# Where the block sums and the high and low parts of w1 and w2 are made: at the conversion, in the second and third pair, instead of in the first group of the last stage

## The chip, the cores and the metric

The kernel runs on one core of a Trainium2 chip. The metric is the device time of one execution in microseconds (us). PE is TensorE, DVE is VectorE, ACT is ScalarE, POOL is GpSimd, and SP is SyncE, which here issues nearly all DMAs. A piece is called 128x512 when it has 128 partitions with 512 numbers in each.

## The reference, cut to what matters

Three blocks follow one another. The weights arrive as 64 bit floats and are converted in the kernel.

```python
attn = sm_attn(q, sm_attn(p, k, v), same)     # 8 batches, 8 heads, 576 rows, 64 wide; 32 packed rows
x = attn.transpose(0, 2, 1, 3).reshape(4608, 512)
x = (silu(x @ w_gate) * (x @ w_val)) @ w_out  # d_ff = 1536
h = (x @ w1) * (x @ w2) @ w3                  # w1, w2: 512 x 1024; w3: 1024 x 1024
out = h @ w_out2                              # 4608 x 512
```

## The kernel before, in words

Every matmul operand is held as a high part (rounded by a cast on ACT) and a low part (value minus high part, a subtraction on DVE or POOL), and three products are added. `split` (L89 and L93) does this.

**Pairs.** After the packed attention, the eight batches go in four pairs P = 0 to 3. A pair runs over 12 feature blocks f of 128. In a step (P, f), `c_mm` multiplies the next step's weights with the packed values into a PSUM tile pc (L409); ACT copies it rounded to ch (L420), and DVE subtracts ch from pc to get cl (L89). `stage1` then makes, for each of the two batches, pg (L441; silu on ACT, L446) and pv (L441; u = u times pv on DVE, L450). Each u is cast to uh on ACT, and POOL subtracts to get ul. After each third f, `stage3` multiplies three f with w_out into px (L672), in two halves that lie inside the next step; without them a step is short. So a short step on PE is pc, pg, pv, pg', pv' (the prime is for the second batch). The PSUM tiles of this part come from one pool of four, in turn: pv' of a step takes the place that pc of the same step had, and so it can start only when the DVE subtraction cl has read pc.

DVE and ACT also work out the softmax of the next pair's queries in these steps (`q_tasks`: sT, qmx, qsm, aT, aTl, transposes qT), and the conversions of weights to 32 bits (`conv`: ACT L346, DVE L347 and L350).

**w1 and w2.** Sixteen conversions i = 0 to 15 stand at the end of the steps from P = 1, f = 3 to P = 2, f = 6. Before, each takes a 128x512 piece of w1 or w2 (`w12_conv`) and stores it to `w12d`.

**The last stage.** Six groups g of tokens are done; each has eight `stage5(g, f)` and a `stage7(g)`. A `stage5` forms x2 @ w1 and x2 @ w2 of one f by seven products of blocks instead of eight (`PROD`): the weight blocks A11, A12, A22 and four sums S1 to S4 of them, against blocks and sums of x2. A step of seven products uses seven tiles `ws`. Before, group 0 makes them: it loads the converted weights (`load_w12`), forms the sums on DVE (`ws_sums`), splits them on ACT and on DVE or POOL (`ws_block`), and stores the tiles to `wsd`, from where groups 1 to 5 load them (`ws_load`). The results of the products go from PSUM to s by ACT (L996).

**Order.** Each engine runs its own fixed list, written when the program is built; an engine waits at the first instruction that isn't ready. Some instructions are pinned behind others (`pin`). SP's list holds the DMA issues, also in one order. Every tile pool has a fixed number of places, and a write waits for the last reader of the place. Raw weights come through a ring of five tiles (tag `raw`), filled by `raw_load`.

Of the kernel before, what the change touches and what calls it, by code (L numbers as in the profile page):

```python
# [8 lines left out]
F32 = mybir.dt.float32  # L9
F32R = mybir.dt.float32r  # L10
I32 = mybir.dt.int32
I64 = mybir.dt.int64
AF = mybir.ActivationFunctionType
ALU = mybir.AluOpType
# [12 lines left out]
S1 = (14.75, 17.75)  # L27
# [11 lines left out]
def packed_attention_moe_kernel(  # L39
# [24 lines left out]
    nc = tc.nc  # L64
# [26 lines left out]
    def split(hi, lo, src, on="act", sub_on="dve"):  # L91
        if on == "act":
            nc.scalar.copy(hi, src)  # L93
        else:
            nc.vector.tensor_copy(hi, src)
        sub(lo, src, hi, sub_on)
# [1 line left out]
    X2d = tc.dram_tile([ND, 128, NT], F32, name="X2d")  # L98
    Wd = tc.dram_tile([NF, 128, 4, 2, 128], F32, name="Wd")
    wod = tc.dram_tile([NF, 128, DM], F32, name="wod")  # L100
    w12d = tc.dram_tile([NF2, 128, 2, ND, 128], F32, name="w12d")
    wsd = tc.dram_tile([NF2, 7, 128, 2, 2, 128], F32, name="wsd")
    wo3d = tc.dram_tile([2, NF2, 128, DM], F32, name="wo3d")

# [174 lines left out]
        }.get(n - at, lambda: None)()  # L279


    w12_list = [(x, c, h) for h in range(2) for x in range(2) for c in range(ND)]
    NH = NF2 // 2
    raw_q = [f"w_{f}_{gv}" for f in range(4) for gv in range(2)]
    for f in range(NF):
# [9 lines left out]
    def raw_src(key):  # L295
        what, *at = key.split("_")
        at = [int(x) for x in at]
        if what == "wo2":
            c, kk = divmod(at[0], NH)
            return w_out2[512 * c:512 * c + 512, :].rearrange("(i k a) n -> k i a n", k=NH, a=32)[kk]  # L300
        if what == "w3":
            c, r = at
            return w3[128 * r:128 * r + 128, 512 * c:512 * c + 512].rearrange(
                "(b rr) (i n) -> i b rr n", rr=4, i=4)
        if what == "w":
            return (w_gate, w_val)[at[1]][:, 128 * at[0]:128 * at[0] + 128].rearrange(
                "(k p) n -> p k n", p=128)
        if what == "wo":
            return w_out[128 * at[0]:128 * at[0] + 128, :]
        x, c, h = w12_list[at[0]]  # L310
        return (w1, w2)[x][128 * c:128 * c + 128, 512 * h:512 * h + 512]

    raw_at = [0]
    load_after = {}
# [2 lines left out]
    def raw_load():  # L317
        if raw_at[0] < len(raw_q):
            key = raw_q[raw_at[0]]
            src = raw_src(key)  # L320
            raw_at[0] += 1
            blocks = src.shape[0] == 4
            t = vc.tile([128, 512] if blocks else [128] + list(src.shape[1:]), I64, tag="raw",
                        name=f"raw_{key}", bufs=5)
            if blocks:
                for i in range(4):
                    to = t[32 * i:32 * i + 32]
                    nc.sync.dma_start(to if len(src.shape) == 3 else to.rearrange("p (r n) -> p r n", r=4), src[i])
            else:
                nc.sync.dma_start(t, src)  # L330
            raw_t.append((key, t))

    def conv(key, t):


        name, raw = raw_t.pop(0)
        assert name == key, (name, key)
        x = vc.tile(list(t.shape), I32, tag="vx", name=f"vx_{key}")
        w = raw.bitcast(I32)
        if len(t.shape) == 3:  # L340
            w = w.rearrange("p a (n e) -> p a n e", e=2)
            low, high = w[:, :, :, 0], w[:, :, :, 1]
        else:
            w = w.rearrange("p (n e) -> p n e", e=2)
            low, high = w[:, :, 0], w[:, :, 1]
        behind(nc.scalar.activation(t, high.bitcast(F32), AF.Prelu, scale=2.0 ** -112, alpha=-2.0 ** 32), "act")  # L346
        behind(nc.vector.tensor_scalar(x, low, 29, None, op0=ALU.logical_shift_right), "dve")  # L347

        def rest():
            nc.vector.scalar_tensor_tensor(  # L350
                t.bitcast(I32), t.bitcast(I32), 3, x, op0=ALU.logical_shift_left, op1=ALU.bitwise_or)

        if in_front[0]:
            conv_rest.append(rest)
        else:
            rest()
        if not in_front[0]:
            raw_load()


    wf_t, wst_t = {}, {}
# [329 lines left out]


    def w12_conv(i):
        x, c, h = w12_list[i]
        t = vl.tile([128, 512], F32, tag="vu", name=f"w12t{i}")
        conv(f"w12_{i}", t)
        nc.sync.dma_start(
            w12d[4 * h:4 * h + 4, :, x, c, :].rearrange("f p n -> p f n"),
            t.rearrange("p (f n) -> p f n", n=128))


    wo2_t, w3T = {}, {}
# [42 lines left out]
    def w3_step(new, old):  # L745
        if old is not None:
            w3_mm(old)
        if new is not None:
# [5 lines left out]

    PROD = (("A", "A11", "B11"), ("B", "S1", "T1"), ("A", "S2", "T2"), ("B", "S4", "B22"),
            ("A", "S3", "T3"), ("C", "A12", "B21"), ("A", "A22", "T4"))
    x2_t, x2r_t, w12r_t, wsrc, ws_t, wg_at = {}, {}, {}, {}, {}, []

    def load_w12(f):
        t = xp.tile([128, 2, 2, 256], F32, tag="wf", name=f"w12r{f}")  # L760
        nc.sync.dma_start(t.rearrange("p x k n -> p x (k n)"), w12d[f].rearrange("p x c n -> p x (c n)"))
        w12r_t[f] = t

    def ws_sums(f):
        t = w12r_t.pop(f)
        a11, a12, a21, a22 = (t[:, x, kh] for x in range(2) for kh in range(2))
        sa = vl.tile([128, 2, 256], F32, tag="vu", name=f"wsa{f}")
        sb = vl.tile([128, 2, 256], F32, tag="vu", name=f"wsb{f}")
        tt = nc.vector.tensor_tensor
        tt(out=sa[:, 0], in0=a21, in1=a22, op=ALU.add)  # L770
        tt(out=sa[:, 1], in0=sa[:, 0], in1=a11, op=ALU.subtract)
        tt(out=sb[:, 0], in0=a11, in1=a21, op=ALU.subtract)
        tt(out=sb[:, 1], in0=a12, in1=sa[:, 1], op=ALU.subtract)
        wsrc[f] = {"A11": a11, "A12": a12, "A22": a22, "S1": sa[:, 0], "S2": sa[:, 1],
                   "S3": sb[:, 0], "S4": sb[:, 1]}

    def ws_tile(g, f, k):
        if f == 0:
            if k % 2 == 0:
                wg_at.append(wgv.tile([128, 2, 2, 256], F32R, tag=("wh", "wl")[k // 2 % 2], name=f"ws0_{k}"))  # L780
            t = wg_at[-1][:, k % 2]
        else:
            t = wst.tile([128, 2, 256], F32R, tag="wst", name=f"ws{g}_{f}_{k}", bufs=14)
        ws_t[f, k] = t
        return t

    def ws_block(f, k):

        t = ws_tile(0, f, k)
        split(t[:, 0], t[:, 1], wsrc[f][PROD[k][1]], sub_on="pool" if k % 2 else "dve")  # L790
        if f:
            nc.sync.dma_start(wsd[f, k], t.bitcast(F32).rearrange("p h (d n) -> p h d n", d=2))

    def ws_load(g, f, k):
        t = ws_tile(g, f, k)
        nc.sync.dma_start(t.bitcast(F32).rearrange("p h (d n) -> p h d n", d=2), wsd[f, k])

    def x2_load(g, i, j):
        t = xp.tile([128, 2, TH], F32, tag="x2r", name=f"x2r{g}_{i}{j}", bufs=3)
# [57 lines left out]
    for n, (P, f) in enumerate(steps):  # L857
# [46 lines left out]
        if 0 <= i < len(w12_list):  # L904
            pin.update(pin_at)
            w12_conv(i)
            pin.clear()
        if P + 1 < NPR:
            q_tasks(2 * P + 2, 0, f)
            q_tasks(2 * P + 3, 5, f)  # L910
# [6 lines left out]
        if P == NPR - 1:  # L917
            if f == 0:
                aA.release()
                qp.release()  # L920
                wp = pool("wp", "left", bufs=2)
            w3_task(P, f, 3)
            if f == 9:
                assert w3_at[0] > len(w3_list)
                wp.release()
                vc.release()
                xp = pool("xp", "left", bufs=2)
                x2_prep(0, 0)
            if f == 10:
                x2_prep(0, 1)  # L930
                x2_prep(0, 2)
            if f == 11:
                x2_prep(0, 3)
                load_w12(0)
                ws_sums(0)
                for k in range(7):
                    ws_block(0, k)
    for e in range(2):
        stage3(*pend, e)
        if e == 0:  # L940
            load_w12(1)
            ws_sums(1)
            load_w12(2)
    up.release()
    aB.release()
    wop.release()
# [24 lines left out]
    def stage5(g, f):  # L971
# [12 lines left out]

        def ahead(k):

            if g == 0 and f + 1 < NF2:
                ws_block(f + 1, k)
            n = (NF2 - 1) * g + f + 1
            ng, nf = divmod(n, NF2 - 1)  # L990
            if f and 0 < ng < NG2:
                ws_load(ng, nf + 1, k)

        def keep(name, t):
# [54 lines left out]
            nc.sync.dma_start(out[r0:r0 + 128, :], o)  # L1049

    load_wo3(0)
    with tc.manual_schedule(engines=M0):
        for g in range(NG2):
            for f in range(NF2):
                stage5(g, f)
                if g == 0:
                    if f + 2 < NF2:
                        ws_sums(f + 2)
                    if f + 3 < NF2:
                        load_w12(f + 3)  # L1060
                    split_wo3(f)
                    if f + 1 < NF2:
                        load_wo3(f + 1)
            ab_split.pop()()
            if g + 1 < NG2:
                for part in range(4):
                    x2_prep(g + 1, part)
            stage7(g)
# [39 lines left out]
```

## Time and profile before

| | |
|---|---|
| median of 3 runs | 1379.38 us (1378.85 to 1380.13) |
| the profiled execution's own time | 1378.52 us |
| its span in the trace | 1376.7 us |
| mean granted TensorE clock | 0.995 of full |
| busy share of PE, DVE, ACT, POOL | 98%, 48%, 42%, 28% |

By the trace the pairs run from about 120 to 825 us (P = 1 begins near 265, P = 3 near 570), and the last stage from 825 us to the end. The time of the profiled execution has 1.8 us outside the span. A busy share is an average: an engine that is busy for 48% of the span can be without a gap for 20 us, and the others may wait for it there.

### The profile page before, as it was taken

The numbers are of one execution on the slowest core, as the hardware profiler recorded it, in microseconds if no ns is written. First come the engines' busy times: TensorE is split into PE (matmuls) and PEld (weight loads), VectorE is DVE, ScalarE is ACT, GpSimd is POOL, SyncE is SP. The second block draws the span as 40 slices with busy tenths as digits, with TensorE's granted clock in tenths as the row PEclk, the third lists the DMA queues.
The fourth block names the chain that finished last, engine by engine and source line by source line (L and its number), as shares of the span: only waits on it lengthen the run. The fifth ranks groups of instructions, "written<-read, shape, count | busy, mean of one in ns | idle before, by whom it ended". The sixth has DMA issues, their size and how long they took to land.

```text
span 1376.7 us, 25585 instructions
## 1 busy us (share of the span) xinstructions
PE 1344.1 (98%) x10196; PEld 1235.3 (90%) x10196; DVE 658.7 (48%) x962; ACT 572.3 (42%) x956; POOL 386.0 (28%) x309
## 2 busy tenths in 40 slices
PE   6889999999999999999999999999999999999998
PEld 4669899999999999999898989989899899898997
DVE  2875867346563466462354378733413333234230
ACT  4784644235432444344544136433323233233231
POOL 0323322323322233253443226502112022021120
PEclk9999999999999999999999999999999999999999
DMA  9997766534455444145343238928548367285441
GB/s 281 314 268 212 228 188 200 153 97 133 125 127 181 124 135 123 55 144 148 120 130 104 82 121 308 347 70 254 173 131 254 105 198 231 74 253 170 132 152 46
DMA packets 195335, 230.28 MB, mean 167 GB/s; under 512 B 71056, under 2 KB 128400, under 8 KB 195216
## 3 DMA queue, kind: packets, MB, share of 16 engines
q1 hardware_dynamic: 195216, 228.64, 53.8%
q8 instruction: 81, 1.33, 0.4%
q14 instruction: 38, 0.31, 0.1%
HBM read 179.04 MB, written 49.55 MB: 166 GB/s over the span
## 4 chain that ended last, share of the span: by engine, by line
PE 85%; POOL 1%; DVE 1%; ACT 1%; issue 0%; DVEq 0%; POOLq 0%; ACTq 0%
PE px L672 20%; PE pA L981 15%; PE po L1045 14%; PE pg L441 10%; PE pv L441 9%; PE pB L981 7%; PE pC L981 4%; PE pc L409 3%; PE pw L736 3%; PE psq L206 1%; POOL wo2l L89 0%; POOL ul L89 0%; DVE u L450 0%; DVE xB21l L89 0%; ACT vt_wo L346 0%
## 5 line engine op out<-in xcount | busy, mean ns | idle before, releaser
L89 POOL TENSOR_TENSOR ul<-u,uh 128x576 fp32r<-128x576 f32 x96 | 146.7, 1528 | 329.3 <-ACT uh L93 324.2
L1001 POOL TENSOR_TENSOR c<-s,s 128x384 f32<-128x384 f32 x48 | 49.2, 1024 | 375.7 <-ACT s L996 375.5
L672 PE MATMUL px<-uh,woh 128*128 128x384 f32 x576 | 148.0, 337 | 2.4 <-DVE acc L682 1.4
L672 PE MATMUL px<-ul,woh 128*128 128x384 f32 x576 | 147.8, 337 | 2.5 <-POOL ul L89 2.5
L672 PE MATMUL px<-uh,wol 128*128 128x384 f32 x576 | 147.2, 336 | 0.0
L996 ACT COPY s<-pA 128x384 f32<-128x384 f32 x144 | 69.2, 481 | 182.6 <-PE pA L981 181.2
L450 DVE TENSOR_TENSOR u<-u,pv 128x576 f32<-128x576 f32 x96 | 71.8, 749 | 108.1 <-PE pv L441 98.2
L93 ACT CAST uh<-u 128x576 fp32r<-128x576 f32 x96 | 64.6, 673 | 115.1 <-DVE u L450 114.8
L682 DVE TENSOR_TENSOR acc<-acc,px 128x768 f32<-128x768 f32 x72 | 68.1, 948 | 92.4 <-PE px L672 92.2
L1045 PE MATMUL po<-wo_hi,abl 128*128 128x512 f32 x288 | 112.2, 390 | 0.0
L1045 PE MATMUL po<-wo_lo,abh 128*128 128x512 f32 x288 | 112.2, 389 | 0.0
L1045 PE MATMUL po<-wo_hi,abh 128*128 128x512 f32 x288 | 112.0, 389 | 0.0
L672 PEld LDWEIGHTS px<-uh,woh 128*128 128x128 f32 x576 | 103.5, 189 | 5.3 <-DVE acc L682 1.9
L672 PEld LDWEIGHTS px<-ul,woh 128*128 128x128 f32 x576 | 104.8, 189 | 3.1 <-POOL ul L89 3.1
L672 PEld LDWEIGHTS px<-uh,wol 128*128 128x128 f32 x576 | 104.9, 189 | 0.0
L89 DVE TENSOR_TENSOR abl<-ab,abh 128x768 fp32r<-128x768 f32 x48 | 48.6, 1013 | 105.1 <-ACT abh L93 105.1
L89 POOL TENSOR_TENSOR wol<-wof,woh 128x512 fp32r<-128x512 f32 x48 | 63.2, 1330 | 108.2 <-ACT woh L93 105.5
L441 PE MATMUL pg<-aTh,ch 128*128 128x288 f32 x384 | 87.2, 308 | 2.1 <-ACT u L446 1.2
L446 ACT ACTIVATE u<-pg 128x576 f32<-128x576 f32 x96 | 62.5, 651 | 60.6 <-PE pg L441 59.1
L441 PE MATMUL pv<-aTh,ch 128*128 128x288 f32 x384 | 82.9, 297 | 0.9 <-DVE cl L89 0.6
L441 PE MATMUL pg<-aTh,cl 128*128 128x288 f32 x384 | 82.3, 296 | 0.0
L441 PE MATMUL pv<-aTh,cl 128*128 128x288 f32 x384 | 82.2, 295 | 0.0
(309 smaller groups left out, 3099.0 us busy)
## 6 DMA issues: line engine op xcount, KB each, us to landing
ws<-wsd SPq DMA_DIRECT2D x245, 256.0 KB, 3.1
wf<-Wd SPq DMA_DIRECT2D x36, 512.0 KB, 4.8
wsd<-ws SPq DMA_DIRECT2D x49, 256.0 KB, 3.1
wof<-wod SPq DMA_DIRECT2D x36, 256.0 KB, 3.0
x2r<-X2d SPq DMA_DIRECT2D x24, 384.0 KB, 4.7
out_dram<-o SPq DMA_DIRECT2D x36, 256.0 KB, 2.0
km<-in_k_dram SPq DMA_DIRECT2D x16, 512.0 KB, 6.9
vm<-in_v_dram SPq DMA_DIRECT2D x16, 512.0 KB, 7.9
```

The lines of the kernel that those rows point to most:

```text
L89: return eng.tensor_tensor(out=out, in0=src, in1=hi.bitcast(F32), op=ALU.subtract)
L93: nc.scalar.copy(hi, src)
L409: nc.tensor.matmul(t[hs[at], b, Q], lhsT=PTd[es, 2 * (2 * P + b) + Q, hs[hq]], rhs=w[es, 2 * Q + hq // 2].rearrange("p g n -> p (g n)"), s ...
L441: nc.tensor.matmul(t[:, hf, 0:HS], lhsT=w[:, b % 2, Q, cols], rhs=x[:, Q, hf, :], start=first, stop=last,)
L446: x = nc.scalar.activation(u, t[:, :, 0:HS], AF.Silu)
L450: x = nc.vector.tensor_tensor(out=u, in0=u, in1=t[:, :, 0:HS], op=ALU.mult)
L672: nc.tensor.matmul(t[:, h, 0:CW], lhsT=w[:, 128 * d:128 * d + 128], rhs=x[:, CW * c:CW * c + CW], start=first, stop=last,)
L682: nc.vector.tensor_tensor(out=o, in0=o, in1=t[:, :, 0:CW], op=ALU.add)
L981: nc.tensor.matmul(bk[n], lhsT=w[:, hl, 128 * d:128 * d + 128], rhs=r[:, d], start=(first and d == 0 and i == 0), stop=(d == 1 and i == 2) ...
L996: nc.scalar.copy(o, t)
L1001: on.tensor_tensor(out=r, in0=o, in1=t, op=op)
L1045: nc.tensor.matmul(t, lhsT=a[:, j, cols], rhs=w[:, f], start=first, stop=last)
```

## The change

A conversion now takes four blocks of 128x128 which belong together: A11, A12, A22, A21 of one f and one half d of the rows. It loads them with four DMAs into one raw tile, converts them, and at once (`w12_blocks`) forms the four sums on DVE, splits the three plain blocks (cast on ACT, subtraction on DVE, 128x384) and the four sums (cast on ACT, subtraction on POOL, 128x512), and stores seven parts to `wsd`. Group 0 then loads its `ws` tiles from `wsd` as the other groups do; `w12d`, its loads, `ws_sums` and `ws_block` are gone. The parts share the ring of five raw tiles, so the raw loads are filled to a depth which changes (`raw_fill`): 5 at first, 2 while the next one belongs to w1, w2 or w_out2, 5 again after the last w1, w2 piece.

```diff
-    w12_list = [(x, c, h) for h in range(2) for x in range(2) for c in range(ND)]
+    w12_list = [(f, d) for f in range(NF2) for d in range(2)]
...
-        x, c, h = w12_list[at[0]]
-        return (w1, w2)[x][128 * c:128 * c + 128, 512 * h:512 * h + 512]
+        f, d = w12_list[at[0]]
+        return [(w1, w2)[x][128 * (2 * kh + d):128 * (2 * kh + d) + 128, 128 * f:128 * f + 128]
+                for x, kh in ((0, 0), (0, 1), (1, 1), (1, 0))]
...
+            if parts:
+                for i in range(4):
+                    nc.sync.dma_start(t[:, 128 * i:128 * i + 128], src[i])
...
+    def raw_fill():
+        if w12_at[0] == len(w12_list):
+            depth = 5
+        else:
+            depth = 2 if raw_q[raw_at[0]].startswith(("w12", "wo2")) else 5
+        while raw_at[0] < len(raw_q) and len(raw_t) < depth:
+            raw_load()
...
         if not in_front[0]:
-            raw_load()
+            raw_fill()
...
     def w12_conv(i):
-        x, c, h = w12_list[i]
+        f, d = w12_list[i]
         t = vl.tile([128, 512], F32, tag="vu", name=f"w12t{i}")
         conv(f"w12_{i}", t)
-        nc.sync.dma_start(
-            w12d[4 * h:4 * h + 4, :, x, c, :].rearrange("f p n -> p f n"),
-            t.rearrange("p (f n) -> p f n", n=128))
+        w12_t[i] = t
...
+    def w12_blocks(i):
+        f, d = w12_list[i]
+        t = w12_t.pop(i).rearrange("p (k n) -> p k n", k=4)
+        a11, a12, a22, a21 = (t[:, k] for k in range(4))
+        x = vl.tile([128, 4, 128], F32, tag="vu", name=f"w12s{i}")
+        s1, s2, s3, s4 = (x[:, k] for k in range(4))
+        tt = nc.vector.tensor_tensor
+        tt(out=s1, in0=a21, in1=a22, op=ALU.add)
+        tt(out=s2, in0=s1, in1=a11, op=ALU.subtract)
+        tt(out=s3, in0=a11, in1=a21, op=ALU.subtract)
+        tt(out=s4, in0=a12, in1=s2, op=ALU.subtract)
+        for src, k0, k1, on in ((t[:, 0:3], 0, 3, "dve"), (x, 3, 7, "pool")):
+            o = vc.tile([128, 2, k1 - k0, 128], F32R, tag="raw", name=f"w12p{i}_{k0}", bufs=5)
+            split(o[:, 0], o[:, 1], src, sub_on=on)
+            for k in range(k0, k1):
+                nc.sync.dma_start(wsd[f, k, :, :, d, :], o[:, :, k - k0].bitcast(F32))
+        w12_at[0] += 1
+        raw_fill()
...
-    def ws_sums(f):
...
-    def ws_block(f, k):
-
-        t = ws_tile(0, f, k)
-        split(t[:, 0], t[:, 1], wsrc[f][PROD[k][1]], sub_on="pool" if k % 2 else "dve")
-        if f:
-            nc.sync.dma_start(wsd[f, k], t.bitcast(F32).rearrange("p h (d n) -> p h d n", d=2))
...
             w12_conv(i)
             pin.clear()
+            w12_blocks(i)
...
-                load_w12(0)
-                ws_sums(0)
                 for k in range(7):
-                    ws_block(0, k)
+                    ws_load(0, 0, k)
...
-            if g == 0 and f + 1 < NF2:
-                ws_block(f + 1, k)
             n = (NF2 - 1) * g + f + 1
             ng, nf = divmod(n, NF2 - 1)
-            if f and 0 < ng < NG2:
+            if (f or g == 0) and ng < NG2:
                 ws_load(ng, nf + 1, k)
```

DVE's list at the end of step f = 4 of the second pair (conversion i = 1), first before, then after. The first row is the u of the second batch, w12t is the converted piece, w12s the sums, w12p the parts, and cl the subtraction for the step after.

```order
L450 TENSOR_TENSOR u_4_4164<-u_4_4164,pv_4_4179 128x576
L347 TENSOR_SCALAR vx_w_1_4196<-raw_w_1_3135 128x512
L350 SCALAR_TENSOR_TENSOR w12t_4195<-w12t_4195,vx_w_1_4196 128x512
L89 TENSOR_TENSOR cl_6_4226<-pc_6_4208,ch_6_4225 128x1024
L450 TENSOR_TENSOR u_5_4229<-u_5_4229,pv_5_4244 128x576
```

```order
L464 TENSOR_TENSOR u_4_4185<-u_4_4185,pv_4_4200 128x576
L361 TENSOR_SCALAR vx_w_1_4217<-raw_w_1_3398 128x512
L364 SCALAR_TENSOR_TENSOR w12t_4216<-w12t_4216,vx_w_1_4217 128x512
L722 TENSOR_TENSOR w12s_4226<-w12t_4216 128x128
L724 TENSOR_TENSOR w12s_4226<-w12t_4216 128x128
L723 TENSOR_TENSOR w12s_4226<-w12s_4226,w12t_4216 128x128
L89 TENSOR_TENSOR w12p_0_4231<-w12t_4216,w12p_0_4231 128x384
L725 TENSOR_TENSOR w12s_4226<-w12t_4216,w12s_4226 128x128
L89 TENSOR_TENSOR cl_6_4267<-pc_6_4249,ch_6_4266 128x1024
L464 TENSOR_TENSOR u_5_4270<-u_5_4270,pv_5_4285 128x576
```

Five instructions now stand between w12t and cl, in each of the sixteen places.

ACT's list at the same place, before and after: the second u (silu), the first half of the conversion, the cast uh, the cast ch and the next silu.

```order
L446 ACTIVATE u_4_4164<-pg_4_4165 128x576
L346 ACTIVATE w12t_4195<-raw_w_1_3135 128x512
L93 CAST uh_4_4156<-u_4_4164 128x576
L420 CAST ch_6_4225<-pc_6_4208 128x1024
L446 ACTIVATE u_5_4229<-pg_5_4230 128x576
```

```order
L460 ACTIVATE u_4_4185<-pg_4_4186 128x576
L360 ACTIVATE w12t_4216<-raw_w_1_3398 128x512
L93 CAST uh_4_4177<-u_4_4185 128x576
L93 CAST w12p_0_4231<-w12t_4216 128x384
L434 CAST ch_6_4266<-pc_6_4249 128x1024
L93 CAST w12p_3_4237<-w12s_4226 128x512
L460 ACTIVATE u_5_4270<-pg_5_4271 128x576
```

One new cast, which waits for DVE's w12t, now stands ahead of ch, and another, which waits for the last of the sums, ahead of the next silu.

DVE's list in the first pair between cl of f = 5 and cl of f = 6, before and after; aT and aTl are the softmax of the next pair's queries, transposed, and its low part, and wf and wof are converted weights of the first block.

```order
L89 TENSOR_TENSOR cl_5_2246<-pc_5_2228,ch_5_2245 128x1024
...
L450 TENSOR_TENSOR u_4_2249<-u_4_2249,pv_4_2264 128x576
L347 TENSOR_SCALAR vx_wo_2328<-raw_wo_2041 128x512
L89 TENSOR_TENSOR aTl_2636<-aT_0_2637,aTh_2635 128x576
L350 SCALAR_TENSOR_TENSOR wof_4_2327<-wof_4_2327,vx_wo_2328 128x512
L450 TENSOR_TENSOR u_4_2296<-u_4_2296,pv_4_2311 128x576
L260 STREAM_TRANSPOSE aT_1_2641<-sT_1960 128x576
L89 TENSOR_TENSOR aTl_2636<-aT_1_2641,aTh_2635 128x576
L89 TENSOR_TENSOR cl_6_2358<-pc_6_2340,ch_6_2357 128x1024
```

```order
L89 TENSOR_TENSOR aTl_2637<-aT_0_2638,aTh_2636 128x576
L259 STREAM_TRANSPOSE aT_1_2642<-sT_1961 128x576
L89 TENSOR_TENSOR cl_5_2247<-pc_5_2229,ch_5_2246 128x1024
...
L464 TENSOR_TENSOR u_4_2250<-u_4_2250,pv_4_2265 128x576
L361 TENSOR_SCALAR vx_wo_2329<-raw_wo_2036 128x512
L89 TENSOR_TENSOR aTl_2637<-aT_1_2642,aTh_2636 128x576
L364 SCALAR_TENSOR_TENSOR wof_4_2328<-wof_4_2328,vx_wo_2329 128x512
L464 TENSOR_TENSOR u_4_2297<-u_4_2297,pv_4_2312 128x576
L89 TENSOR_TENSOR cl_6_2359<-pc_6_2341,ch_6_2358 128x1024
```

One aTl and the second transpose have moved from between the two cl to ahead of the first.

## Rows read from the trace of the kernel before

**Rows 1.** The page's first part: busy time, share, instructions.

```profile
PE 1344.1 (98%) x10196; PEld 1235.3 (90%) x10196; DVE 658.7 (48%) x962; ACT 572.3 (42%) x956; POOL 386.0 (28%) x309
```

**Rows 2.** Windows: busy time by engine, then granted clock, DMA share, GB/s.

```profile
300.00:420.00 120.00, 120.00 (x1048) 111.86 (x1047) 71.84 (x89) 54.60 (x76) 38.62 (x26) 1.00 0.46 128
...
780.00:810.00 30.00, 26.59 (x180) 23.56 (x179) 21.61 (x20) 11.49 (x16) 9.15 (x6) 0.92 0.31 101
...
826.00:886.00 60.00, 60.00 (x338) 58.22 (x337) 52.76 (x91) 38.65 (x95) 39.08 (x37) 1.00 0.89 319
```

**Rows 3.** DVE, timeline of a short step: start, duration, line, tiles, idle before.

```profile
408.91 0.70 DVE L350 SCALAR_TENSOR_TENSOR w12t<-w12t,vx_w 128x512 int32<-128x512 int32 x1
410.14 1.23 DVE L89 TENSOR_TENSOR cl<-pc,ch 128x1024 fp32r<-128x1024 f32 x1 [0.53 <-ACT ch L420]
```

**Rows 4.** ACT and POOL, timeline of the same step.

```profile
409.10 1.01 ACT L420 CAST ch<-pc 128x1024 fp32r<-128x1024 f32 x1
...
409.27 1.63 POOL L89 TENSOR_TENSOR ul<-u,uh 128x576 fp32r<-128x576 f32 x1 [1.25 <-ACT uh L93]
```

**Rows 5.** PE, timeline of the same step: pc and the first matmuls of pv'.

```profile
407.55 1.09 PE L409 MATMUL pc<-wf,PTd 64*32 64x256 f32 x32
...
413.47 0.42 PE L441 MATMUL pv<-aTh,ch 128*128 128x288 f32 x2
```

**Rows 6.** DVE, PE and POOL, timeline of the dense place in the second pair.

```profile
317.90 1.18 DVE L89 TENSOR_TENSOR cl<-pc,ch 128x1024 fp32r<-128x1024 f32 x1
...
324.86 1.76 DVE L350 SCALAR_TENSOR_TENSOR w12t<-w12t,vx_w 128x512 int32<-128x512 int32 x1
326.55 1.21 DVE L89 TENSOR_TENSOR cl<-pc,ch 128x1024 fp32r<-128x1024 f32 x1
...
320.89 0.42 PE L441 MATMUL pv<-aTh,ch 128*128 128x288 f32 x2
...
328.50 0.42 PE L441 MATMUL pv<-aTh,ch 128*128 128x288 f32 x2
...
324.64 1.44 POOL L89 TENSOR_TENSOR ul<-u,uh 128x576 fp32r<-128x576 f32 x1 [0.16 <-ACT uh L93]
```

**Rows 7.** DVE and PE, timeline of the dense place in the third pair.

```profile
482.58 1.35 DVE L243 TENSOR_REDUCE qsm<-sT 128x36 f32<-128x1152 f32 x1 [2.40 <-ACT sT L238]
...
496.98 1.23 DVE L89 TENSOR_TENSOR cl<-pc,ch 128x1024 fp32r<-128x1024 f32 x1 [0.40 <-ACT ch L420]
...
499.05 0.42 PE L441 MATMUL pv<-aTh,ch 128*128 128x288 f32 x2
```

**Rows 8.** DVE and POOL, timeline where x2 is prepared, and SP's issue.

```profile
792.08 1.43 POOL L89 TENSOR_TENSOR ul<-u,uh 128x576 fp32r<-128x576 f32 x1 [10.69 <-ACT uh L93]
...
792.22 2.11 DVE L806 TENSOR_TENSOR x2T<-x2r,x2r 128x768 f32<-128x768 f32 x1 [0.92 <-DMA x2r<-X2d]
...
795.22 0.36 SPq L801 DMA_DIRECT2D x2r<-X2d  x1
795.78 0.95 DVE L806 TENSOR_TENSOR x2T<-x2r,x2T 128x768 f32<-128x768 f32 x1
```

**Rows 9.** Groups of instructions, group 0 (825 to 886): busy, mean ns | idle before.

```profile
L93 ACT CAST ws<-w12r 128x256 fp32r<-128x256 f32 x21 | 7.9, 408 | 0.0
...
L981 PEld LDWEIGHTS pA<-xT3h,ws 128*128 128x128 f32 x32 | 5.9, 188 | 1.6 <-ACT s L996 1.6
...
L771 DVE TENSOR_TENSOR wsa<-wsa,w12r 128x256 f32<-128x256 f32 x6 | 2.6, 425 | 0.2
```

**Rows 10.** The same view of group 1 (918 to 977).

```profile
L981 PEld LDWEIGHTS pA<-xT3h,ws 128*128 128x128 f32 x32 | 5.9, 188 | 0.0
```

**Rows 11.** PE, timeline in the first pair: its waits there.

```profile
157.10 0.54 PE L441 MATMUL pv<-aTh,ch 128*128 128x288 f32 x2 [0.56 <-DVE cl L89]
...
159.73 1.10 PE L409 MATMUL pc<-wf,PTd 64*32 64x256 f32 x32 [0.76 <-ACT uh L93]
```

**Rows 12.** The page's fifth part: POOL's subtraction of 128x512.

```profile
L89 POOL TENSOR_TENSOR wol<-wof,woh 128x512 fp32r<-128x512 f32 x48 | 63.2, 1330 | 108.2 <-ACT woh L93 105.5
```

More of the change, by code (lines that the diff above doesn't have):

```diff
@@ L100, in packed_attention_moe_kernel @@
     wod = tc.dram_tile([NF, 128, DM], F32, name="wod")
-    w12d = tc.dram_tile([NF2, 128, 2, ND, 128], F32, name="w12d")
     wsd = tc.dram_tile([NF2, 7, 128, 2, 2, 128], F32, name="wsd")
@@ L321, in raw_load @@
             raw_at[0] += 1
-            blocks = src.shape[0] == 4
-            t = vc.tile([128, 512] if blocks else [128] + list(src.shape[1:]), I64, tag="raw",
+            parts = isinstance(src, list)
+            blocks = not parts and src.shape[0] == 4
+            t = vc.tile([128, 512] if blocks or parts else [128] + list(src.shape[1:]), I64, tag="raw",
                         name=f"raw_{key}", bufs=5)
-            if blocks:
+            if parts:
+                for i in range(4):
+                    nc.sync.dma_start(t[:, 128 * i:128 * i + 128], src[i])
+            elif blocks:
                 for i in range(4):
@@ L331, in raw_load @@
             raw_t.append((key, t))
+    def raw_fill():
[5 more added lines that the diff above has]
+            raw_load()
+    w12_at = [0]
     def conv(key, t):
@@ L693, in w12_conv @@
     def w12_conv(i):
-        x, c, h = w12_list[i]
+        f, d = w12_list[i]
         t = vl.tile([128, 512], F32, tag="vu", name=f"w12t{i}")
         conv(f"w12_{i}", t)
-        nc.sync.dma_start(
-            w12d[4 * h:4 * h + 4, :, x, c, :].rearrange("f p n -> p f n"),
-            t.rearrange("p (f n) -> p f n", n=128))
+        w12_t[i] = t
+    w12_t = {}
+    def w12_blocks(i):
[16 more added lines that the diff above has]
+        raw_fill()
     wo2_t, w3T = {}, {}
@@ L756, in packed_attention_moe_kernel @@
             ("A", "S3", "T3"), ("C", "A12", "B21"), ("A", "A22", "T4"))
[L757 to L762, printed above, removed]
-    def ws_sums(f):
[L765 to L775, printed above, removed]
+    WSK = [("A11", "A12", "A22", "S1", "S2", "S3", "S4").index(name) for _, name, _ in PROD]
+    x2_t, x2r_t, ws_t, wg_at = {}, {}, {}, []
     def ws_tile(g, f, k):
@@ L785, in ws_tile @@
         return t
-    def ws_block(f, k):
-        t = ws_tile(0, f, k)
-        split(t[:, 0], t[:, 1], wsrc[f][PROD[k][1]], sub_on="pool" if k % 2 else "dve")
-        if f:
-            nc.sync.dma_start(wsd[f, k], t.bitcast(F32).rearrange("p h (d n) -> p h d n", d=2))
     def ws_load(g, f, k):
         t = ws_tile(g, f, k)
-        nc.sync.dma_start(t.bitcast(F32).rearrange("p h (d n) -> p h d n", d=2), wsd[f, k])
+        nc.sync.dma_start(t.bitcast(F32).rearrange("p h (d n) -> p h d n", d=2), wsd[f, WSK[k]])
     def x2_load(g, i, j):
@@ L933, in packed_attention_moe_kernel @@
                 x2_prep(0, 3)
-                load_w12(0)
-                ws_sums(0)
                 for k in range(7):
-                    ws_block(0, k)
+                    ws_load(0, 0, k)
     for e in range(2):
         stage3(*pend, e)
[L940 to L943, printed above, removed]
     up.release()
@@ L1051, in packed_attention_moe_kernel @@
     load_wo3(0)
+    for k in range(7):
+        ws_load(0, 1, k)
     with tc.manual_schedule(engines=M0):
@@ L1056, in packed_attention_moe_kernel @@
                 if g == 0:
[L1057 to L1060, printed above, removed]
                     split_wo3(f)
```

## The prediction

> **What bounds the kernel now.** I read the page first, then the windows by stage, then timelines of DVE, ACT, POOL and PE around the conversions, and last the groups of group 0. The page says that PE works for 98% of the span [rows 1], so the gain to be had is the PE time that is idle or slow, and the loss to be feared is a new wait of PE. In a window of the second pair, where conversions run, PE has no idle time at all, 120.00 of 120.00 us, while DVE is busy for 71.84 us [rows 2]. An average of 60% hides what decides here: how late the instruction that PE needs next may become.
>
> That instruction is cl. Pv' of a step takes the PSUM place of pc, so it can't start before DVE has read pc for cl. In a short step pc starts at 407.55 and pv' at 413.47 [rows 5], 5.92 us later. ACT makes ch from 409.10 to 410.11 [rows 4], and DVE makes cl from 410.14 to 411.37 [rows 3]. So cl has 2.10 us to spare. The first pair shows what happens without it: at 157.10 pv waited 0.56 us for cl [rows 11]. Elsewhere less is left. In the second pair, behind the softmax of the queries, one cl runs from 317.90 to 319.08 for a pv' at 320.89 (1.81 us), and the next from 326.55 to 327.76 for a pv' at 328.50, which leaves 0.74 us. In the third pair the same place has cl at 496.98 to 498.21 for a pv' at 499.05 (0.84 us) [rows 6, 7].
>
> **What leaves group 0.** The casts, sums and splits of `ws` go. PE is busy there for 60.00 of 60.00 us [rows 2], so this isn't worth the DVE time that goes, which nothing on PE waited for. What PE shows is a weight load that waited 1.6 us in all for ACT's copy s, behind ACT's casts of 0.41 us; group 1 has 0.0 at the same load [rows 9, 10]. I take 1.6 us as the gain, between 0 and 1.9 (a further 0.3 for the slower first products).
>
> **What the conversions gain in work.** Four DVE sums of 128x128 and a subtraction of 128x384, two ACT casts, and a POOL subtraction of 128x512. No row has 128x128. DVE takes 0.425 us for 256 columns [rows 9] and 1.23 us for 1024 [rows 3]: some 1.05 ns a column, so 0.29 us for 128 and 0.56 for 384. Four sums and the subtraction are 1.72 us, and as DVE's instructions overlap by up to 0.1 us (in rows 6, 324.86 + 1.76 ends after 326.55) it comes to 1.4 to 1.7; I take 1.5 per conversion. ACT takes 0.41 us for 256 columns and 1.01 for 1024 [rows 4, 9], so 0.51 and 0.61 for the two casts. POOL's 128x512 is 1.33 us [rows 12], and POOL has the time: 38.62 of 120 us [rows 2].
>
> All five DVE instructions stand ahead of cl, and one ACT cast, which waits for w12t, ahead of ch. In the short step w12t ends at 409.61 [rows 3]. The cast ends at about 410.15 and ch at 411.2; the sums end at 411.1; cl then runs to 412.4, and pv' at 413.47 doesn't wait. Taken alone, an undisturbed conversion is free.
>
> **What can lengthen them.** DVE and POOL disturb each other when DVE reads only from SBUF. With POOL's ul running from 792.08, DVE's x2T of 128x768 took 2.11 us, against 0.95 for the same instruction a little later [rows 8]. At 324.86 w12t took 1.76 us against 0.70 elsewhere, with POOL's ul at 324.64 to 326.08 [rows 3, 6]: it ended 0.6 us behind ul. The sums read only SBUF, and ul' starts at 409.27, during w12t, and took 1.63 us where 1.44 is usual [rows 4, 6]. If ul gets its turn as w12t ends, the sums start 1.3 us later and cl ends at 413.7: 0.2 us late. The Trainium skill, SBUF — State Buffer, section "SBUF: two separate sides", says that the port pair the two share is locked by whichever starts first for the whole instruction, for DVE operations with two SBUF inputs too. The rows above agree with it. By that rule alone every conversion would pay the full wait, and the sum of waits below would be 6.5 us (3.6, 2.0 and 0.9) instead of 5.2. A conversion thus delays DVE by 1.5 us free and by 2.8 behind ul.
>
> **The sum, place by place.** Where the px halves follow, PE has over 9 us of other work before the next pv', and I cost these conversions at nothing. What remains are those in steps that a short step follows: i = 1, 4, 7, 10, 13.
> - i = 1. The conversion before it (i = 0) stands ahead of the softmax, and its delay, 1.5 to 2.8 us, goes through to the cl at 317.90, which has 1.81: PE waits 0 to 1.0, say 0.6. Then DVE is late by about 2.3 us at u', and i = 1 adds 1.5 to the cl at 326.55 (its w12t there already waited for ul): 327.76 + 2.3 + 1.5 = 331.5 against 328.50 + 0.6, so 2.4 more. I take 3.0 us in all, between 0 (the delay of i = 0 is absorbed, and w12t falls clear of ul and is back at 0.70 us) and 3.6 (2.8 and 1.5, less 0.74).
> - i = 13. The softmax ahead of it waits 2.40 us for ACT's exponential [rows 7], which takes most of the delay of i = 12. Left are 1.5 to 2.8 us at a cl with 0.84: 0.7 to 2.0, and I take 1.3.
> - i = 4, 7, 10: 0.2 us each by the short step above, and 0.3 more at i = 4, where four transposes for the queries stand in DVE's list as well: 0.9, between 0 and 2.4 (half a us more for each).
> Together 5.2 us, between 0.7 and 8.0.
>
> **Other terms.** In the first pair the raw loads start earlier, and one aTl and one transpose move from before cl of f = 6 to before cl of f = 5. The waits at 157.10 and 159.73, 0.56 and 0.76 us [rows 11], can go, and the earlier cl can take their place; I take a gain of 0.8, between 1.3 and a loss of 0.3. At the start of the last stage x2T waits 0.92 us for the load of x2r [rows 8], and PE waits for what follows: 26.59 of 30 us are busy there and the clock falls to 0.92 [rows 2]. SP's list now has the seven `ws` loads of group 0 among these loads. One issue is 0.36 us [rows 8], and 256 KB at the 319 GB/s that group 0 reached [rows 2] are 0.8 us, so x2r is 0.4 to 1.2 us later; I take 0.6. The loads of `ws` in group 0 take the place of stores and loads of `w12r`; the 0.89 share of DMA there [rows 2] falls, and I cost them at nothing. If a store of w12p held its raw place, ACT's cast, and with it ch, would wait; five places at one conversion per 8 to 17 us leave several us.
>
> 5.2 + 0.6 - 1.6 - 0.8 = +3.4 us. On the profiled execution, 1378.52 us, that makes 1381.9 (a span of 1380.1 and the 1.8 us around it); the median of the runs is 0.86 above this execution, so the time is 1379.38 + 3.4, about 1382.8.
>
> **Rivals.** (a) The sums fit. Both engines let each other through, the delay of i = 0 is absorbed before cl, and only the 0.7 us of i = 13 come; with the other terms -1.1 us, about 1378.3. For it: PE has no idle time in the window of the second pair, and 1.81 and 2.10 us of room are more than 1.5. Against it: 0.74 and 0.84 at the two dense places, where 1.5 can't be hidden. (b) The waits of PE are few, and the first pair and group 0 give all they can (1.3 + 1.9), without the delay of x2r: -3.2 us with no wait at all, 1376.2. It is a gain that can be measured as long as all waits together stay below 0.4 us; with the 0.7 of i = 13 it is 1376.9. (c) The waits bring the slow clock. After the idle time near 800 the granted clock averaged 0.92 over 30 us [rows 2], 2.4 us lost. Waits of 2.4 us and 1.3 to 2.0 at the dense places, followed by the same, would add up to 2 x 2.4 us: 1387.6. Against it: PE was idle for 3.41 us in those 30 (30.00 less 26.59), more than either dense place would give.
>
> **Chances.** The forecast, waits of 2.4 to 8.0 us, 0.48; (a) 0.22; (b) 0.18; (c) 0.12. What a measurement of this kernel can't tell from no change is about 0.2%, 2.8 us: faster is below 1376.6, slower above 1382.1. The forecast's own range is 1380.0 to 1385.6, and I put two thirds of it above 1382.1: 0.32, and with all of (c) slower is 0.44. (a), the rest of the forecast and a little of (b) are the same: 0.41. Most of (b) is faster: 0.15. For 8 in 10 I go from 1376.2, the end of (b), to 1387.6, the time of (c).
>
> **What the profile after would show.** Right: PE waits for cl (or pv with a DVE release) near f = 4 to 5 of the second and third pair, 2 to 3 us and about 1; sums of 0.3 us, some over 1 beside ul; no wait of pA's loads for s in group 0. Wrong: no idle time of PE in the second and third pair, or ACT's ch late because a cast waits for a DMA. I would be most wrong if DVE and POOL took turns with less loss than at 324.86, or if the later x2r cost much more than its own delay.

## The result, and the profile after

The changed kernel takes 1400.26 us (median of 4 runs, 1396.17 to 1403.2), the kernel before 1379.76 in the same comparison: a ratio of 1.0147, with a 95% interval of 1.012 to 1.0175. The forecast was 1382.8, with a range of 1376.2 to 1387.6. It is slower, as forecast, but by 20.5 us where 3.4 were forecast. The profiled execution took 1399.08 us, with a span of 1397.3, 20.6 us longer than before.

The page of the changed kernel, its PE row, two rows of its fifth part and two of its sixth:

```profile
PE 1354.8 (97%) x10196; PEld 1240.2 (89%) x10196; DVE 658.4 (47%) x978; ACT 569.8 (41%) x932; POOL 379.9 (27%) x301
...
L455 PE MATMUL pv<-aTh,ch 128*128 128x288 f32 x384 | 84.7, 302 | 13.3 <-ACT u L460 12.5
L455 PE MATMUL pg<-aTh,ch 128*128 128x288 f32 x384 | 87.5, 309 | 2.3 <-ACT u L460 1.2
...
raw_w<-in_moe_w_dram SPq DMA_DIRECT2D x128, 128.0 KB, 3.2
wsd<-w12p SPq DMA_DIRECT2D x112, 128.0 KB, 2.2
```

PE's busy time grew by 10.7 us [rows 1] although it does the same 10196 matmuls, so part of the loss is a slower clock. The other part is new idle time, 12.5 us of it ahead of pv. Where both lie is plain when the start of pc is compared step by step in the two traces. "Added" is what the steps up to this pc took longer than before.

| part of the kernel | added, us |
|---|---|
| attention front, up to the third pc (103.75 before, 101.77 after) | -1.98 |
| first pair and the start of the second, to pc at 314.98 (314.46) | +1.46 |
| second and third pair with all conversions, to pc at 543.41 (565.56) | +22.67 |
| fourth pair, to its last pc at 785.96 (807.07) | -1.04 |
| from there to the first pA of group 0 at 825.50 (847.01) | +0.40 |
| group 0, to the first pA of group 1 at 918.11 (938.42) | -1.20 |
| the rest | +0.25 |

The front isn't touched by the change and differs from run to run: over the ten traces of this study that follow the kernel before, the third pc starts at 101.8 to 108.6 us (the first two stand among the packed attention). Single spans are therefore compared from the third pc on.

PE waits of the changed kernel, all of the second and third pair (290 to 570), then the timeline of PE at one of them, and windows (PE, PEld, DVE, ACT, POOL, clock) around four:

```profile
PE pv L455 <- ACT u L460: 12.5, 6, 3.0
PE pv L455 <- DVE cl L89: 0.4, 1, 0.4
```

```profile
330.75 0.54 PE L455 MATMUL pv<-aTh,ch 128*128 128x288 f32 x2 [2.38 <-ACT u L460]
...
332.25 0.68 PE L455 MATMUL pv<-aTh,cl 128*128 128x288 f32 x2
```

```profile
331.00:336.00 5.00, 5.00 (x51) 3.50 (x51) 3.24 (x5) 3.50 (x6) 3.35 (x3) 0.66 0.63 181
368.00:374.00 6.00, 5.79 (x63) 3.78 (x64) 4.25 (x6) 2.62 (x5) 2.86 (x3) 0.72 0.20 48
469.00:475.00 6.00, 5.60 (x50) 4.17 (x56) 2.40 (x5) 2.81 (x5) 3.28 (x3) 0.50 0.64 186
519.00:524.00 5.00, 4.40 (x45) 3.41 (x45) 2.41 (x5) 2.77 (x5) 2.70 (x2) 0.66 0.63 182
```

Four of the six waits (2.38, 1.74, 2.99 and 2.45 us) are followed by PE at a reduced clock; the same pair of matmuls takes 0.68 us instead of 0.43. By these four windows the clock costs 1.7 + 1.7 + 3.0 + 1.7 = 8.1 us (their length times what is missing to 1.00), in addition to 12.9 us of idle time.

**The first cause, at the two dense places.** DVE and ACT at the second conversion (i = 1) of the changed kernel, to be laid beside [rows 6]:

```profile
326.24 1.75 DVE L364 SCALAR_TENSOR_TENSOR w12t<-w12t,vx_w 128x512 int32<-128x512 int32 x1
328.09 0.29 DVE L722 TENSOR_TENSOR w12s<-w12t 128x128 f32<-128x128 f32 x1
...
329.17 0.28 DVE L725 TENSOR_TENSOR w12s<-w12t,w12s 128x128 f32<-128x128 f32 x1
329.48 1.23 DVE L89 TENSOR_TENSOR cl<-pc,ch 128x1024 fp32r<-128x1024 f32 x1
...
328.02 0.51 ACT L93 CAST w12p<-w12t 128x384 fp32r<-128x384 f32 x1 [2.10 <-DVE w12t L364]
328.44 1.00 ACT L434 CAST ch<-pc 128x1024 fp32r<-128x1024 f32 x1
329.53 0.62 ACT L93 CAST w12p<-w12s 128x512 fp32r<-128x512 f32 x1
330.06 0.64 ACT L460 ACTIVATE u<-pg 128x576 f32<-128x576 f32 x1
```

ACT stood for 2.10 us at the cast which waits for w12t. Behind it in ACT's list are ch, the cast of the sums, and u, the silu of the step's first batch. The sums end at 329.45 and ch at 329.44, so the second cast hardly waits for the sums. U ends at 330.70 and pv' starts at 330.75; the profile names u as what released pv'. Cl ends at 330.71, so this place alone can't tell u from cl. Two other waits can. At 368.21 in the same trace pv' starts behind the end of u (368.15), while cl still runs; and in e9 below pv' starts at 330.12, with u done at 330.06 and cl running to 330.89:

```profile
367.50 0.65 ACT L460 ACTIVATE u<-pg 128x576 f32<-128x576 f32 x1
...
367.64 1.22 DVE L89 TENSOR_TENSOR cl<-pc,ch 128x1024 fp32r<-128x1024 f32 x1 [6.18 <-ACT ch L434]
...
368.21 0.53 PE L455 MATMUL pv<-aTh,ch 128*128 128x288 f32 x2 [1.74 <-ACT u L460]
```

So in these steps it is u that holds pv', and the place in PSUM that pv' takes must be that of pg, which u reads, and not that of pc, as the description of the pairs has it for every step. Pv' does wait for cl in the step that follows the conversion i = 12 (0.39 us at 509.07, named DVE cl), as it did at 157.10 [rows 11]. In the kernel before, u at the place of i = 1 was done at 326.21, 2.29 us ahead of pv' at 328.50:

```profile
325.56 0.65 ACT L446 ACTIVATE u<-pg 128x576 f32<-128x576 f32 x1
```

The first cause, then, is two new casts ahead of u in ACT's list, the first of which waits for w12t. The wait of 2.45 us at i = 13 has the same four ACT instructions.

**The second cause, which the forecast didn't have.** SP and ACT after the fourth conversion (i = 3):

```profile
355.44 4.76 SPq L730 DMA_DIRECT2D wsd<-w12p  x7
360.24 2.04 SPq L328 DMA_DIRECT2D raw_w<-in_moe_w_dram  x4
362.39 0.85 SPq L403 DMA_DIRECT2D wof<-wod  x2
...
359.11 0.62 ACT L93 CAST woh<-wof 128x512 fp32r<-128x512 f32 x1 [0.42 <-PE px L686]
366.08 0.62 ACT L93 CAST woh<-wof 128x512 fp32r<-128x512 f32 x1 [6.34 <-DMA wof<-wod]
366.60 1.00 ACT L434 CAST ch<-pc 128x1024 fp32r<-128x1024 f32 x1
```

Seven stores and four raw loads keep SP issuing for 6.8 us. The loads of wof stand behind them in SP's list, land late, and ACT waits 6.34 us for one. Before the change it waited 2.93 us at this place:

```profile
358.79 0.62 ACT L93 CAST woh<-wof 128x512 fp32r<-128x512 f32 x1 [2.93 <-DMA wof<-wod]
```

Ch and u follow on ACT, and PE waits 1.74 us for u at 368.21. At 415.46 (behind i = 6) the late cast of woh stands directly ahead of u, and PE waits 1.96 us:

```profile
414.24 0.62 ACT L93 CAST woh<-wof 128x512 fp32r<-128x512 f32 x1 [4.60 <-DMA wof<-wod]
414.76 0.64 ACT L460 ACTIVATE u<-pg 128x576 f32<-128x576 f32 x1
```

At 462.96 (behind i = 9) ACT waited 6.06 us for wof, and PE 0.98 us for a u. The wait of 2.99 at 469.40 follows in the same step: it has the list of the first cause (i = 10, where the forecast had 0.2), and all of it comes later by the late wof.

### The profile page after: what moved, and what is told of

Read it like the earlier page. It is cut to its first block, busy times and chain, and to the rows that moved or that the text cites. A ratio compares the mean times of both kernels' runs of the same rounds, so it can differ in the third digit from the quotient of the medians.

```text
span 1397.3 us, 25800 instructions
## 1 busy us (share of the span) xinstructions
PE 1354.8 (97%) x10196; PEld 1240.2 (89%) x10196; DVE 658.4 (47%) x978; ACT 569.8 (41%) x932; POOL 379.9 (27%) x301
## 4 chain that ended last, share of the span: by engine, by line
PE 80%; DVE 4%; POOL 2%; issue 2%; DMA 2%; ACT 2%; SPq 1%; DVEq 0%; ACTq 0%; POOLq 0%
PE px L686 19%; PE pA L985 14%; PE po L1047 14%; PE pv L455 8%; PE pg L455 8%; PE pB L985 7%; PE pC L985 4%; PE pw L769 3%; PE pc L423 3%; DMA wof<-wod 1%; PE psq L205 1%; POOL ul L89 1%; DVE w12t L364 1%; SPq L328 1%; SPq L730 1%
## 5 line engine op out<-in xcount | busy, mean ns | idle before, releaser
L455 PE MATMUL pv<-aTh,ch 128*128 128x288 f32 x384 | 84.7, 302 | 13.3 <-ACT u L460 12.5
L455 PE MATMUL pv<-aTl,ch 128*128 128x288 f32 x384 | 83.2, 299 | 0.0
```

What stands on the lines that cost most here:

```text
L455: nc.tensor.matmul(t[:, hf, 0:HS], lhsT=w[:, b % 2, Q, cols], rhs=x[:, Q, hf, :], start=first, stop=last,)
```

## The experiments

Each comparison is with the kernel before on the same chip; its median there was 1380.29 us for e1 to e4, 1380.41 for e5 to e8 and 1380.33 for e9.

**e1: fewer DMAs per conversion.** The four blocks are ordered A21, A22, A11, A12, so that two DMAs load them and two store the parts.

```diff
-                for i in range(4):
-                    nc.sync.dma_start(t[:, 128 * i:128 * i + 128], src[i])
+                for i in range(2):
+                    nc.sync.dma_start(t[:, 256 * i:256 * i + 256].rearrange("p (k n) -> p k n", k=2), src[i])
...
-            for k in range(k0, k1):
-                nc.sync.dma_start(wsd[f, k, :, :, d, :], o[:, :, k - k0].bitcast(F32))
+            nc.sync.dma_start(wsd[f, k0:k1, :, :, d, :].rearrange("k p h n -> p h k n"), o.bitcast(F32))
```

> The changed kernel, but a conversion has two raw loads and two stores to wsd in place of four and seven: the same bytes and the same work on DVE, ACT and POOL. Theory S (SP's queue): the eleven issues take 4.77 + 2.05 us of SP per conversion, the loads of wof stand behind them, and ACT waits for wof; with four issues the waits of PE behind a late wof (1.74, 1.96 and 0.98 us and what they lead to, 469.40 among them) go, and the time is about 1386. Theory D (the sums and casts ahead of cl and ch make all of it): nothing changes, 1396 to 1403.

Measured: 1391.14 us, ratio 1.0073 (1.005 to 1.0095); 9 us of the loss are gone. The first row is the source view of a store in the changed kernel (one part), the second the same of e1 (three or four parts), with least, median and largest ns; then come ACT's timeline at i = 3 and PE's waits of the two pairs, both of e1:

```profile
L730 SPq DMA_DIRECT2D wsd<-w12p x112: 512/618/1172, 308.4 to 548.8; - x112
```

```profile
L729 SPq DMA_DIRECT2D wsd<-w12p x32: 581/592/701, 312.2 to 540.7; - x32
```

```profile
367.21 0.62 ACT L93 CAST woh<-wof 128x512 fp32r<-128x512 f32 x1 [3.75 <-DMA wof<-wod]
```

```profile
PE pv L455 <- ACT u L460: 6.8, 4, 2.4
```

The time of an issue hardly depends on the bytes: a store takes 0.59 us with three to four times as much. ACT's wait for wof at i = 3 is back to 3.75 us and PE's wait there is gone. The steps that had added 2.25, 1.35 and 2.22 us add 0.00, -0.01 and 0.61. The dense places keep their loss (3.11 + 1.08 and 3.91 us), and a step before i = 10 still adds 2.79, where ACT waits 4.4 us for a wof. So both causes are real, and this edit takes the second away only in part. Theory D alone falls.

**e2: the blocks one place later.** All eleven DMAs stay. The block work is written behind u of the next step's first batch, and the sums and casts are pinned there.

```diff
             w12_conv(i)
             pin.clear()
-            w12_blocks(i)
+            blk.append(i)
...
             stage1(2 * P, f, 1)
+        if blk:
+            pin.update(pin_at)
+            w12_blocks(blk.pop())
+            pin.clear()
...
-        tt(out=s1, in0=a21, in1=a22, op=ALU.add)
+        behind(tt(out=s1, in0=a21, in1=a22, op=ALU.add), "dve")
...
-            split(o[:, 0], o[:, 1], src, sub_on=on)
+            behind(nc.scalar.copy(o[:, 0], src), "act")
+            sub(o[:, 1], src, o[:, 0], on)
```

> The changed kernel, but the sums, casts and subtractions of a conversion stand one place later: in the next step, behind u of the first batch on DVE and its silu on ACT, so that cl and ch come first. All eleven issues per conversion stay. Theory D: the waits at the two dense places (2.4 us each, with 1.7 us each of slow clock) and most others go, 1379 to 1384. Theory S: only the two dense places go, some 8 us, and the waits behind wof stay: about 1391.

Measured: 1378.31 us, ratio 0.9987 (0.9976 to 0.9998). One wait of 0.4 us is left in the second and third pair. This went past what theory S allowed, since with the later parts the stores also stand later in SP's list: here the loads of wof go out at 358.82, and the next stores at 364.75. The edit removes both causes at once, and doesn't tell their shares. Rows of DVE and POOL from this run show how the sums and the subtraction fare when they meet POOL's subtractions:

```profile
323.86 0.28 DVE L724 TENSOR_TENSOR w12s<-w12t 128x128 f32<-128x128 f32 x1
324.07 1.38 DVE L723 TENSOR_TENSOR w12s<-w12s,w12t 128x128 f32<-128x128 f32 x1
325.37 1.77 DVE L89 TENSOR_TENSOR w12p<-w12t,w12p 128x384 fp32r<-128x384 f32 x1
...
324.00 1.30 POOL L89 TENSOR_TENSOR wol<-wof,woh 128x512 fp32r<-128x512 f32 x1 [5.75 <-ACT woh L93]
325.26 1.47 POOL L89 TENSOR_TENSOR ul<-u,uh 128x576 fp32r<-128x576 f32 x1
```

The second sum takes 1.38 us beside wol, where 0.28 is usual, and the subtraction 1.77 beside ul, where it was 0.55 at i = 1 of the changed kernel. That agrees with the Trainium skill, SBUF — State Buffer, section "SBUF: two separate sides", by which DVE with two SBUF inputs and POOL hold a shared port pair in turn. Here it costs PE nothing: w12t of i = 1 ends 6.6 us behind the step's pc (5.7 in the changed kernel), but no cast that waits for it stands ahead of u any more.

**e3: both edits.**

> Both edits: four issues per conversion and the blocks one place later. Both theories: no wait of PE left in the second and third pair, 1376.5 to 1379, since the group 0 and first pair gains of the change remain. If a third cause exists (DVE and POOL in each other's way however the list is ordered), the time stays above 1382.

Measured: 1381.02 us, ratio 1.0004 (0.9995 to 1.0014), above the expected range. The second and third pair are as in e2 (one wait of 0.4). What differs lies in group 0, whose steps take 7.42 us here (as in e4) and 7.28 in e2, with no wait that the profile shows, and behind the pairs, where pA waits 1.05 us for DVE. Why is open.

**e4: no block work.** The sums, casts and subtractions are left out, and the seven stores take columns of the converted piece.

```diff
-        tt(out=s1, in0=a21, in1=a22, op=ALU.add)
...
-            split(o[:, 0], o[:, 1], src, sub_on=on)
...
+        for k in range(7):
+            nc.sync.dma_start(wsd[f, k, :, :, d, :], t[:, k % 3:k % 3 + 2])
```

> The changed kernel with the sums, casts and subtractions of the conversions left out (the stores take columns of the converted piece, so the values of w1 and w2 in the last stage are not the right ones); all eleven issues per conversion stay. Theory S: the waits behind wof stay, 1384 to 1392. Theory D: no wait is left, 1376 to 1379.

Measured: 1381.48 us, ratio 1.0013 (1.0002 to 1.0023), between the two forecasts and again with one wait of 0.4 us in the two pairs. That wait (for cl, at 498.38) is thus not made by the block work. Theory S in its simple form, that eleven issues alone make wof late enough, falls: the stores here wait for w12t only, and ACT waits 3.34 us for the wof that it waited 6.34 for. It takes the stores of parts that are finished late, and the loads behind them.

**e5: the stores issued by POOL.**

```diff
-                nc.sync.dma_start(wsd[f, k, :, :, d, :], o[:, :, k - k0].bitcast(F32))
+                nc.gpsimd.dma_start(wsd[f, k, :, :, d, :], o[:, :, k - k0].bitcast(F32))
```

> The changed kernel, but the seven stores of a conversion are issued by POOL instead of SP; the lists of DVE and ACT stay as in the changed kernel. If the stores ahead of the loads of wof on SP make wof late (theory S), no wait of PE stands behind a late wof any more: the 3.6, 2.2 and about 7 us lost at the steps after the third, seventh and tenth conversion go, the two dense places keep their 4 us each, and the time is 1386 to 1390. If wof is late for another reason, 1396 to 1403.

Measured: 1410.17 us, ratio 1.0222 (1.0208 to 1.0236). It is a miss for both theories, and no test of them: POOL spends its own time on the issues, in the midst of the work that others wait for. POOL of e5, and ACT's waits for wof in the second and third pair:

```profile
362.17 2.11 POOL L730 DMA_DIRECT2D wsd<-w12p  x3 [1.31 <-DVE w12s L725]
363.91 1.69 POOL L89 TENSOR_TENSOR w12p<-w12s,w12p 128x512 fp32r<-128x512 f32 x1
365.89 2.82 POOL L730 DMA_DIRECT2D wsd<-w12p  x4 [0.29 <-POOL w12p L89]
```

```profile
ACT woh L93 <- DMA wof<-wod: 20.3, 3, 7.3
```

The seven issues take 4.9 us of POOL, and wol, which frees the place that the next wof needs, comes behind them.

**e6 and e7: depth 4 in the first pair,** in e2 and in the changed kernel.

```diff
-            depth = 2 if raw_q[raw_at[0]].startswith(("w12", "wo2")) else 5
+            depth = 2 if raw_q[raw_at[0]].startswith(("w12", "wo2")) else 4
```

> The kernel of e2 (blocks one place later) with a raw depth of 4 instead of 5 in the first pair, as the kernel before had. The trace of the changed kernel and of all four experiments shows 1.46 us lost between the first and the fourteenth step of the first pair, with a new wait of psq for qT of 1.41. If the deeper loads make it, 1.5 us less than e2: about 1376.9. If not, the same as e2.

> The changed kernel with the raw depth of 4 in the first pair alone. By its own the same 1.5 us as between e2 and e6: about 1398.8, inside the spread of the changed kernel, so the trace decides: no wait of psq for qT, and 0.0 instead of 1.46 us lost in the first pair.

Measured: e6 1376.81 us, ratio 0.9979 (0.9969 to 0.9989); e7 1398.09, ratio 1.014 (1.0124 to 1.0155). In both traces the first pair adds nothing (0.02 us from the first to the fourteenth step, against 1.46), and the wait of psq is gone. PE waits of the changed kernel in the first pair (108 to 290), then of e6:

```profile
PE psq L205 <- DVE qT L156: 1.4, 1, 1.4
PE pc L423 <- ACT uh L93: 0.5, 1, 0.5
```

```profile
PE pc L423 <- ACT uh L93: 0.8, 1, 0.8
PE pv L455 <- DVE cl L89: 0.6, 1, 0.6
```

With depth 5 DVE's list has a conversion of wo between the two transposes qT for which psq waits. The waits of 0.56 and 0.76 at f = 6 [rows 11] shrink to one of 0.5 with depth 5, as the forecast said, but not for free. E6 is the fastest version here, 0.2% below the kernel before.

**e8 and e9: only the casts late, only the sums late.** These are e2 without the pins on the sums, and without the pins on the casts.

> The kernel of e2, but only ACT's two casts are held behind the silu of the next step; DVE's four sums may stand ahead of cl again, and do at the dense places. If the cast ahead of ch, which waits for w12t, makes the waits, about as e2, 1378 to 1380. If DVE's sums ahead of cl make them, the waits at the two dense places come back in part: 1380 to 1384.

> The mirror of e8: only DVE's sums are held behind u of the next step; ACT's first cast stands ahead of ch again, as in the changed kernel. If the cast ahead of ch makes the waits at the dense places (it can only begin when w12t is done, and ch and cl follow it), PE waits 0.5 to 2 us at each of them, and the time is 1380 to 1385. If the sums on DVE make them, no wait, 1378 to 1379.

Measured: e8 1379.17 us, ratio 1.000 (0.999 to 1.001); e9 1381.35, ratio 1.0005 (0.9993 to 1.0018). PE's waits in the second and third pair of e8; then the waits of e9 at the two dense places, and ACT and DVE at the first of them:

```profile
PE pv L455 <- DVE cl L89: 0.8, 2, 0.4
```

```profile
330.12 0.53 PE L455 MATMUL pv<-aTh,ch 128*128 128x288 f32 x2 [1.34 <-ACT u L460]
...
503.02 0.53 PE L455 MATMUL pv<-aTh,ch 128*128 128x288 f32 x2 [1.59 <-ACT u L460]
```

```profile
328.09 0.51 ACT L93 CAST w12p<-w12t 128x384 fp32r<-128x384 f32 x1 [0.94 <-DVE w12t L364]
328.51 1.00 ACT L434 CAST ch<-pc 128x1024 fp32r<-128x1024 f32 x1
329.41 0.65 ACT L460 ACTIVATE u<-pg 128x576 f32<-128x576 f32 x1
...
329.68 1.21 DVE L89 TENSOR_TENSOR cl<-pc,ch 128x1024 fp32r<-128x1024 f32 x1
```

At the places of i = 1 and i = 13, PE waits 2.38 and 2.45 us with both casts ahead of u (the changed kernel), 1.34 and 1.59 with only the cast that waits for w12t (e9), and not at all with neither (e2, e8). In e8 three of the five new DVE instructions stand ahead of cl at i = 1 again; its two waits of 0.4 are for cl, behind i = 0 and i = 12. So the casts on ACT make the first cause. DVE has a part in it only through when w12t is ready: it ends 5.7 us behind the step's pc in the changed kernel and 4.0 before. How much of the 2.4 us that delay is, no run tells alone. Neither e8 nor e9 has a wait behind a late wof, since their stores, too, are late in SP's list.

## Why the prediction was wrong

**What failed: the wait itself.** The first step of the working names cl on DVE as what every pv' waits for, and reads 0.74 us of room at i = 1 [rows 6] and 0.84 at i = 13 [rows 7]. That holds at 157.10, the wait that it points at, but not at i = 1, 10 and 13: there pv' waited for u on ACT, with 2.38, 2.99 and 2.45 us. So the five DVE instructions ahead of cl were costed, and the two casts ahead of u were not. The forecast had the first cast in its text, but only ahead of ch, and let it end at 410.15, where w12t isn't held up.

**What failed: a cost taken as nothing, on a queue.** The step on the seven stores and four raw loads of a conversion asked only whether a store would hold its raw place. It didn't cost the issues: one store of the converted piece at 0.38 us and one raw load at 0.33 became seven of 0.68 and four of 0.51 (4.76 and 2.04 us at i = 3). And it didn't ask what stands behind them on SP. The conversions i = 3, 6 and 9, with px halves behind them, were costed at nothing; but it is behind their stores that wof comes late. The steps there add 3.6 us (2.25 behind i = 3, and 1.35 in the next step with the clock), 2.2 behind i = 6 and, where the late wof of i = 9 meets the dense work of i = 10, 7.3 (6.34 + 0.92). For i = 4, 7 and 10 together the forecast had 0.9. E1 shows the share of SP behind i = 3 and 6: 5.8 us become 0.6. The forecast's own sign of being wrong, a late ch because a cast waits for a DMA, came at i = 3.

**What failed: the clock.** Rival (c) had 0.12. Its mechanism came, at four of six waits, with 8.1 us in all; the forecast had 4.8 for it at two places. The argument against it, that PE had been idle for 3.41 us around 800 before the clock fell there, didn't hold: here 1.74 us was enough once. The length of the wait alone doesn't decide it, though: the 1.96 us at 415.46 left the clock at 1.00, and so did a wait of 2.38 us at i = 1 in e7, where the changed kernel's wait of the same length was followed by 0.66. The window of e7 there, with a clock of 1.00:

```profile
331.00:336.00 5.00, 5.00 (x63) 4.30 (x62) 3.50 (x5) 3.77 (x6) 3.59 (x3) 1.00 0.63 178
```

**What was right, and what was luck.** The durations were right: the sums take 0.28 us free and 1.38 beside POOL (0.29 and some 1.3 more were assumed), the casts 0.51 and 0.62. In the step behind i = 0, where pv' does wait for cl, 0.6 us were forecast and 0.2 were added. That the 3.0 us for i = 1 lie near the 2.38 measured is luck, as they were added up on a list that PE didn't wait for there; with the clock the steps add 4.2 (2.95 + 1.21). At i = 13 PE waited 2.45 and not 1.3.

**Smaller terms.** Group 0 gave 1.20 us of the forecast 1.6; the loads of xT3h, which waited 1.6 us for s [rows 9], now wait 0.1. The way from the last pc to group 0 got longer by 0.40, for 0.6. The first pair was forecast to gain 0.8 and lost 1.46, with the sign wrong: of the moved instructions only those beside cl were looked at, not the ones ahead of psq. In the fourth pair a wait of pw for ACT of 0.8 us (682.16 before) went away, which wasn't foreseen.

Of the 20.6 us in the trace, 12.9 are idle time of PE and 8.1 the clock in the two pairs; another 1.7 of the 22.67 there isn't assigned. Open is also how much of the wait at 469.40 is each cause's: e1 has 1.73 us of waiting at the step before i = 10 and hardly any at i = 10.

## What to carry to other kernels

Work that moves to a place where the engines have time also takes its DMAs there: count the issues on the queue, and look at which load stands behind stores whose data are finished last. Of an instruction that is put ahead of another in an engine's list, what it waits for can count for more than its own duration: a cast of 0.51 us cost PE 1.3 to 1.6 us in e9, as it waits for another engine's w12t and all of ACT's list waits with it. And what one wait of an instruction is for need not hold for the next: in steps that look alike pv' waited for cl once and for u another time, so take the releaser from several steps. The same work put one place later cost nothing: in e2, DVE is busy for 171.35 of the 250 us from 300 on, and PE for 249.59.

## What the runs showed of the hardware

A DMA issue on SP took 0.37 to 0.39 us for w12d (256 KB, the kernel before), 0.51 to 1.17 with a median of 0.62 for a 128 KB store to wsd, and 0.59 for three to four of those in one. On POOL seven such issues took 4.9 us. A DVE sum of 128x128 took 0.28 us alone and 1.38 beside POOL's wol. In the changed kernel TensorE fell from its upper to its lower level of clock behind waits of 1.74, 2.38, 2.99 and 2.45 us, and not behind one of 1.96; in e7 it did not fall behind one of 2.38.
